# One attention and MLP kernel: the decay's shift moved into the exponential, its rows made and sent in another way, and an accumulation reordered

## The chip, the cores and the metric

The kernel runs on one core of one Trainium2 chip. The metric is device time in microseconds (us) of one execution; lower is better. A core has five engines that run their own instruction queues side by side: TensorE (PE, with its weight loads as PEld), VectorE (DVE), ScalarE (ACT), GpSimd (POOL) and SyncE (SP, which here only issues DMA transfers). They wait for each other by semaphores. Matrix results go to PSUM, a memory of eight banks; everything else lives in SBUF, 128 partitions wide.

## The reference

A "forgetting" attention is followed by a two-layer MLP. There are 8 batches, 8 heads, 576 positions and 64 features a head.

```python
log_f = np.log(np.clip(f, 0.0001, 1.0))
cum = np.cumsum(log_f, axis=-1)
decay = cum[:, :, :, None] - cum[:, :, None, :]
scores = np.where(causal, -1e9, q @ k.T / 8 + decay)      # per batch and head
attn = softmax(scores)
x = (attn @ v) as (4608, 512)                             # heads side by side
h = x @ w_in                                              # 512 -> 2048
out = (h - np.tanh(h)) @ w_out                            # 2048 -> 512, float32
```

The softmax is computed without its maximum: a fixed SHIFT of 5.0 is subtracted from each score ahead of the exponential instead, and it cancels in the division.

## The kernel before, in words

**Decay inside the matmul.** The score tile is K-rows times Q-columns, contracted over the 64 features. The decay is added by three more contraction rows: K carries a high part of 8·cum (rounded to fp16), the low part that the rounding left, and ones; Q carries minus one, minus one, and 8·cum - 40 (the 40 is 8·SHIFT). After the scale of 1/8 in the exponential that gives score + cum(i) - cum(j) - 5. So `QT` and `KT`, the operands of one batch, have D + 3 = 67 rows for each head; two sets of them alternate between batches.

**How the rows are made.** `f` is read in as 64 rows, one for each batch and head (L138), and a second time as 24 rows, three for each head of batch 0 (L139). VectorE clips them (L185), ScalarE takes the logarithm (L192), VectorE scans the prefix sums (`cum`, L195), then makes the high part `chi` (L197) and the low part. Per-row factors that pick high, low and one come from small operations on columns of an identity (`per`, L179 to L191). `cq`, ScalarE's 8·cum - 40 (L585), is the row for Q. From `chi`, `clo` and `cq` the rows are sent by DMA into `KT` and `QT`: by GpSimd's queue for batch 0 (`bulk`, L219 to L221), by SyncE's for the others (`load_aug`, L207); rows of plus and minus one are sent by SyncE too (`const_rows`).

**Pair 0.** Heads are worked on in pairs, 4 to a batch. The first pair cannot wait for those transfers. It has operands of its own, `KS` and `QS`, which borrow the space of later weights (`W1`, `W2`): 64 features and the 24 rows, 88 in all, written in place by the engines. For head 0, L198 writes K's rows and `row_q(0, ...)` (L580) the Q rows; head 1 gets a copy of K's rows (L593) and a second `row_q`, with other factors that pick its three rows of the 24.

**Start.** `start()` writes out by hand the order around it. TensorE first runs dummy matmuls on a constant tile (`unread`), then transposes q and k of pair 0 (`trans`, L304), then more dummies up to the first score tile (L358). Each transposed pair is copied from PSUM to SBUF in four parts (q by ScalarE, L315; k by VectorE, L317), so that head 0's two parts can come first. Each score tile is masked by a matmul with `late` in batch 0 (L361), and ScalarE's exponential (L367) takes it out of PSUM. There are seven tiles in a pair: 0 to 2 for the first head, 3 for the last keys of both heads, 4 to 6 for the second. `bulk()` then gives GpSimd its loads in order: q and k of heads 4 and 5, the three row transfers, q and k of heads 6 and 7, and v.

**After that.** `att_items(p)` gives the order of steps for each pair p: score tiles, transposes for the next pair, the products with v of the pair before (`values`, L395, with VectorE's division into `xn`), and for batch 1 on a DMA transpose of `xn` into `XR` (L429, L431), the transposed attention. MLP steps are dealt out in between by fixed counts: `mlp1` (L457) is one tile of 128 hidden features for a unit of 512 tokens, followed by ScalarE's tanh (L462) and VectorE's `gq` (L468). Of the nine units the first has a plain second layer (`mlp2_plain`, L498): a bank holds two blocks m of 128 tokens by 256 outputs; each block is summed in two steps of eight feature tiles, the first and the second half of the 2048. The order of its 16 steps is e (output half), mp (pair of token blocks), m, half. The other units save a multiplication of blocks by sums and differences (`mlp2`, L523). Engines run their instructions strictly in the written order; nothing is rescheduled. Each DMA queue of GpSimd takes eight transfers at a time: the ninth issue waits for the landing of the first.

Of the kernel before, what the change touches and what calls it, by code (L numbers as in the profile page):

```python
# [8 lines left out]
FP32 = mybir.dt.float32  # L9
FP16 = mybir.dt.float16  # L10
# [4 lines left out]
PITCH = 640  # L15
# [6 lines left out]
def kernel(  # L22
# [137 lines left out]
    clo = cst.tile([NH, S], FP16)  # L160
    cq = cst.tile([NH, S], FP16)
    KS = W1.rearrange("p k e -> p (k e)")[:, 0:2 * PITCH].rearrange("p (a n) -> p a n", a=2)
    QS = W2.rearrange("p k e -> p (k e)")[:, 0:2 * S].rearrange("p (a n) -> p a n", a=2)
    nc.vector.memset(KS[0:NX, :, S:PITCH], 0.0)
    per = cst.tile([NX, 9], FP32)
    nc.vector.memset(vn[0][D:P, NJ - 1, :, :], 0.0)
    isb, isc, mul_k, add_k, mul_l, mul_0, add_0, mul_1, add_1 = (per[:, i:i + 1] for i in range(9))
# [7 lines left out]
    def column(g, h):  # L175
        return id16[0:NX, NH + 3 * h + g:NH + 3 * h + g + 1]
# [11 lines left out]
    for h, (mul, add) in enumerate(((mul_0, add_0), (mul_1, add_1))):  # L188
        nc.vector.tensor_scalar_mul(out=mul, in0=column(1, h), scalar1=inv_qscale)
        nc.vector.scalar_tensor_tensor(out=add, in0=mul, scalar=-SHIFT, in1=column(0, h), op0=ALU.mult, op1=ALU.add)  # L190
        nc.vector.tensor_tensor(out=add, in0=add, in1=column(2, h), op=ALU.subtract)  # L191
# [6 lines left out]
    nc.vector.scalar_tensor_tensor(out=KS[NH:NX, 0, 0:S], in0=cum[NH:NX, :], scalar=mul_l[NH:NX, :], in1=chi[NH:NX, :],  # L198
                                   op0=ALU.mult, op1=ALU.subtract)

    def aug_rows(b):
        i, hs = b % 2, slice(b * H, (b + 1) * H)
        return [(KT[i][D:D + 1, :, 0:S], chi[hs, :]), (KT[i][D + 1:D + 2, :, 0:S], clo[hs, :]), (QT[i][D + 2:D + 3, :, :], cq[hs, :])]
# [5 lines left out]
    def const_rows(i):  # L209
        nc.sync.dma_start(out=QT[i][D:D + 2, :, :], in_=minus16)  # L210
        nc.sync.dma_start(out=KT[i][D + 2:D + 3, :, 0:S], in_=ones16[0:H, :])
# [3 lines left out]
    def bulk():  # L215
        (k_hi, chi_0), (k_lo, clo_0), (q_hi, cq_0) = aug_rows(0)
        load_qk(qn, q, 0, 4, 6)
        load_qk(kn, k, 0, 4, 6)
        nc.gpsimd.dma_start(out=k_hi, in_=chi_0)  # L219
        nc.gpsimd.dma_start(out=q_hi, in_=cq_0)  # L220
        nc.gpsimd.dma_start(out=k_lo, in_=clo_0)  # L221
# [121 lines left out]
    def scores(b, c, ti):  # L343
# [10 lines left out]
        kt, qt, rows = (KS, QS, NX) if b == 0 and c == 0 else (KT[b % 2], QT[b % 2], D + 3)  # L354
# [12 lines left out]
        nc.scalar.activation(out=e[:, lo:hi], in_=ps[:, lo:hi], func=AF.Exp, scale=qscale)  # L367
# [124 lines left out]
    def mlp2_plain(u, s):  # L492
        e, mp, m, half = s // 8, s // 4 % 2, s // 2 % 2, s % 2
# [82 lines left out]
    REST = []  # L576

    def start():
        def row_q(h, mul, add):
            nc.scalar.activation(out=QS[NH:NX, h, :], in_=cum[NH:NX, :], func=AF.Identity, bias=add[NH:NX, :], scale=mul[NH:NX, :])  # L580

        unread(47)
        row_q(0, mul_0, add_0)
        q_rest = trans(*pairs[0], qn, (QS,), True, "AAAA", True)
        nc.scalar.activation(out=cq, in_=cum[0:NH, :], func=AF.Copy, bias=-SHIFT * inv_qscale, scale=inv_qscale)  # L585
# [6 lines left out]
        nc.vector.scalar_tensor_tensor(out=clo, in0=cum[0:NH, :], scalar=inv_qscale, in1=chi[0:NH, :], op0=ALU.mult, op1=ALU.subtract)  # L592
        nc.vector.tensor_copy(out=KS[NH:NX, 1, 0:S], in_=KS[NH:NX, 0, 0:S])  # L593
# [13 lines left out]
    def att_items(p):  # L607
# [8 lines left out]
        for ti in range(len(TILES)):  # L616
# [5 lines left out]
            if p == 0 and ti in (0, 2, 5, 6):  # L622
                put(unread, {0: 2, 2: 14, 5: 4, 6: 6}[ti])
# [103 lines left out]
```

## Time and profile before

| | |
|---|---|
| median of 3 runs | 341.31 us (341.13 to 341.52) |
| the profiled execution's own time | 341.6 us |
| its span, first to last instruction | 339.9 us |
| granted TensorE clock | 1.00 |
| VectorE busy, share of the span | 77% |
| ScalarE busy | 69% |
| GpSimd busy | 48% |
| transfers in GpSimd's queue | 18.39 MB in 94592 packets |

The profile is of one execution. Instructions are grouped by line, engine and operation; a row of the timeline has its start, its duration, the engine, the line, what it writes and reads, how many instructions are merged, and in brackets how long the engine was idle before and what ended that. In the list of waits each row gives the total, how often, and the longest. The chain of waits is followed back from the last instruction; each piece has its start and length. In a stretch's row the first two numbers are its bounds and length, followed by busy time (and instruction count) of PE, PEld, DVE, ACT and POOL, the granted clock, the time the DMA engines were busy, and the rate. For DMA issues the last number is the median time from issue to landing. For one tile, a row gives the least, median and greatest of these times.

### The profile page before, as it was taken

The page shows a single profiled execution, that of the slowest core. Times are in us where ns is not written, and L with a number is a line of the kernel's source. Part 1 is how long each engine was busy: PE and PEld are TensorE (multiplying, and loading weights), DVE is VectorE, ACT ScalarE, POOL GpSimd, SP SyncE. Part 2 cuts the span into 40 slices and gives each one's busy share as a digit, 9 for nine tenths or more (in the row PEclk, how much of TensorE's full clock was granted, in tenths as well). Part 3 has the DMA queues.
Part 4 walks back from the last instruction along what each step waited for, and adds up shares of the span by engine and source line. Part 5 has one row for each costly group of instructions (what it writes and reads, how often), then busy time and mean ns, then how long its engine had stood idle before and what let it go on. Part 6 is the DMA issues. An engine that isn't in the chain of part 4 may idle for free.

```text
span 339.9 us, 8804 instructions
## 1 busy us (share of the span) xinstructions
PE 333.0 (98%) x3345; PEld 237.7 (70%) x3345; DVE 262.5 (77%) x516; ACT 235.1 (69%) x440; POOL 163.7 (48%) x323
## 2 busy tenths in 40 slices
PE   8999999999999999999999999999999999999995
PEld 8775557875588558855788888656875686486485
DVE  8898986659888888678967886688668766966864
ACT  6998777878987886778677867787558743632630
POOL 8894765885657573677377647632322210000000
PEclk9999999999999999999999999999999999999999
DMA  9999999999959999999999999990130023002003
GB/s 116 124 173 201 187 198 179 153 162 196 137 93 181 159 116 92 136 168 130 106 106 191 131 110 112 165 133 15 49 115 13 17 62 101 0 31 95 1 16 109
DMA packets 147535, 38.88 MB, mean 114 GB/s; under 512 B 128221, under 2 KB 146381, under 8 KB 147493
## 3 DMA queue, kind: packets, MB, share of 16 engines
q0 software_dynamic: 94592, 18.39, 74.1%
q1 hardware_dynamic: 52868, 19.88, 31.7%
q8 instruction: 26, 0.43, 0.5%
q14 instruction: 17, 0.13, 0.2%
q10 hardware_dynamic: 32, 0.06, 0.0%
HBM read 36.90 MB, written 9.44 MB: 136 GB/s over the span
## 4 chain that ended last, share of the span: by engine, by line
PE 85%; DVE 8%; DMA 2%; ACT 2%; issue 1%; ACTq 0%
PE hps L457 35%; PE ops L523 29%; PE ps L358 11%; PE av L395 7%; DMA XR<-xn 2%; PE ops L498 2%; DVE KT L317 2%; DVE QT L317 1%; ACT e L367 1%; DVE gq L468 1%; PE t L304 1%; DVE xn L406 1%; DVE W L317 1%; PE x L423 0%; DVE TQ L195 0%
## 5 line engine op out<-in xcount | busy, mean ns | idle before, releaser
L457 PE MATMUL hps<-XR,win 128*128 128x512 f16 (+1 forms) x640 | 140.9, 357 | 0.5 <-DMA XR<-xn 0.3
L462 ACT ACTIVATE th<-hps 128x512 f32<-128x512 f32 x144 | 86.6, 602 | 55.5 <-PE hps L457 52.8
L367 ACT ACTIVATE e<-ps 128x512 f16<-128x512 f32 x192 | 110.5, 598 | 9.8 <-PE ps L358 7.9
L468 DVE TENSOR_TENSOR gq<-hps,th 128x512 f16<-128x512 f32 x144 | 98.1, 687 | 24.2 <-ACT th L462 22.6
L377 POOL TENSOR_SCALAR_AFFINE_SELECT e<-e 128x128 f16<-128x128 f16 x168 | 60.3, 362 | 69.9 <-ACT e L367 67.9
L457 PEld LDWEIGHTS <-win 128*128 128x128 f16 x640 | 57.7, 97 | 48.7 <-issue 0.7
L358 PE MATMUL ps<-QT,KT 67*128 67x512 f16 (+1 forms) x372 | 73.8, 277 | 0.8 <-ACT e L367 0.4
L523 PEld LDWEIGHTS <-gq 128*128 128x128 f16 x640 | 60.2, 97 | 11.2
L523 PE MATMUL ops<-wout,gq 128*128 128x256 f16 x512 | 63.2, 272 | 0.0
L358 PEld LDWEIGHTS <-KT 67*128 67x128 f16 x372 | 35.3, 98 | 22.2 <-issue 1.2
L395 PEld LDWEIGHTS <-e 128*128 128x128 f16 x896 | 32.3, 97 | 3.6
L395 PE MATMUL av<-vn,e 128*128 128x65 f16 x896 | 33.6, 193 | 0.0
L131 POOL DMA_DIRECT2D vn<-in_v_dram x32 | 28.0, 878 | 7.5 <-DMA win<-in_moe_w_in_dram 3.4
L523 PE MATMUL ops<-W,sq 128*128 128x256 f16 x256 | 31.2, 272 | 0.0
L406 DVE TENSOR_TENSOR xn<-av,rs 128x640 f16<-128x640 f32 x32 | 26.4, 825 | 1.1
L523 PEld LDWEIGHTS <-sq 128*128 128x128 f16 x256 | 24.1, 97 | 3.4
L108 POOL DMA_DIRECT2D qn<-in_q_dram x25 | 21.1, 845 | 3.7 <-DMA wout<-in_moe_w_out_dram 1.9
L377 POOL TENSOR_SCALAR_AFFINE_SELECT el<-el 128x128 f16<-128x128 f16 x28 | 9.4, 337 | 26.9 <-ACT el L367 26.7
L108 POOL DMA_DIRECT2D kn<-in_k_dram x25 | 21.1, 845 | 1.5 <-issue 1.1
L404 DVE TENSOR_SCALAR rs<-av 128x10 f32<-128x10 f32 x32 | 5.2, 162 | 18.1 <-PE av L395 17.0
L498 PE MATMUL ops<-wout,gq 128*128 128x256 f16 x128 | 16.9, 272 | 0.4 <-DVE gq L468 0.3
L317 DVE COPY QT<-t 64x576 f16<-64x576 f16 x18 | 14.4, 801 | 3.5 <-PE t L304 3.4
(93 smaller groups left out, 321.0 us busy)
## 6 DMA issues: line engine op xcount, KB each, us to landing
out_dram<-ost SPq DMA_DIRECT2D x34, 256.0 KB
vn<-in_v_dram POOLq DMA_DIRECT2D x24, 128.0 KB, 5.6
qn<-in_q_dram POOLq DMA_DIRECT2D x20, 128.0 KB, 4.9
kn<-in_k_dram POOLq DMA_DIRECT2D x20, 128.0 KB, 5.0
win<-in_moe_w_in_dram POOLq DMA_DIRECT2D x2, 1024.0 KB, 12.3
wout<-in_moe_w_out_dram POOLq DMA_DIRECT2D x2, 1024.0 KB, 17.0
XR<-xn SPq DMA_TRANSPOSE x56
qn<-in_q_dram POOLq DMA_DIRECT2D x6, 144.0 KB, 4.7
```

What stands on the lines that cost most here:

```text
L108: nc.gpsimd.dma_start(out=dst[b % 2][0:pn, n, :].rearrange("p (h d) -> p h d", h=H), in_=src[b, :, n * P:n * P + pn, :].rearrange("h p d - ...
L131: nc.gpsimd.dma_start(out=vn[b % 2][:, n, h0:h1, 0:D], in_=v[b, h0:h1, n * P:(n + 1) * P, :].rearrange("h p d -> p h d"))
L317: nc.vector.tensor_copy(out=to, in_=of)
L358: nc.tensor.matmul(out=ps[:, col:col + n], lhsT=kt[0:rows, h, j * P:(j + 1) * P], rhs=qt[0:rows, h, i0:i0 + n], start=True, stop=cut == 0)
L367: nc.scalar.activation(out=e[:, lo:hi], in_=ps[:, lo:hi], func=AF.Exp, scale=qscale)
L377: nc.gpsimd.affine_select(out=view, in_=view, compare_op=ALU.is_ge, fill=0.0, base=0, pattern=pat, channel_multiplier=-1)
L395: nc.tensor.matmul(out=av[:, a, ib, :], lhsT=E.pop((b, c, a, j, ib)), rhs=vn[b % 2][:, j, 2 * c + a, 0:D + 1], start=(j == 0), stop=(j == ib))
L406: nc.vector.tensor_tensor(out=xn.rearrange("p i (a d) -> p a i d", a=2), in0=av[:, :, :, 0:D], in1=rs.to_broadcast([P, 2, NJ, D]), op=ALU. ...
L457: nc.tensor.matmul(out=hps[:, o:o + n], lhsT=win[:, ci, ft * P:(ft + 1) * P], rhs=XR[:, ci, t:t + n], start=(ci == 0), stop=(ci == NCH - 1))
L462: nc.scalar.activation(out=th, in_=hps, func=AF.Tanh, scale=-1.0)
L468: nc.vector.tensor_tensor(out=GQ[(u, i)][:, half, kt, :], in0=hps, in1=th, op=ALU.add)
L523: nc.tensor.matmul(out=ps[:, m, :], lhsT=LHS[lhs](u, kt // 4)[:, kt % 4, m * P:(m + 1) * P], rhs=rhs[:, kt, :], start=(fresh and (apart or ...
```

## The change

- SHIFT goes out of the Q rows and into the exponential, as a bias of -5.0 given as a number. Q's decay row is then 8·cum, and its fp16 form is K's high part `chi`: `cq` is dropped, and `chi` is sent to `QT` as well.
- The 24 extra rows of `f` become three, all of batch 0's head 0: partitions 64, 65 and 66 hold K's high, low and one row where `KT` wants them. The low parts of all rows are made by one operation (`clo`, 67 rows), and three rows of it are copied to head 0 of `KT`. `KS`, `QS` and the second `row_q` go; pair 0 uses `KT[0]` and `QT[0]`. Head 1 of pair 0, like heads 2 to 7, now gets its rows by DMA.
- `bulk` sends the three rows ahead of q and k of heads 4 and 5.
- All four q copies of pair 0 stand in ScalarE's queue ahead of the first exponential.
- Dummy matmuls between score tiles: 4, 4, 2 and 14 become 2 and 6.
- `mlp2_plain` runs both token blocks over the first half of the features before the second half.

```diff
-    NX = NH + 3 * H
+    NX = NH + 3
-    nc.scalar.dma_start(out=lf[NH:NX, :], in_=bass.AP(f.tensor, f.offset, [[S, H], [0, 3], [1, S]]))
+    nc.scalar.dma_start(out=lf[NH:NX, :], in_=bass.AP(f.tensor, f.offset, [[0, 3], [1, S]]))
...
-    for to, g in ((isb, 1), (isc, 2)):
-        nc.vector.tensor_reduce(out=to, in_=id16[0:NX, NH + g:NX:3], op=ALU.add, axis=mybir.AxisListType.X)
-    nc.vector.tensor_scalar(out=mul_k, in0=isb, scalar1=-inv_qscale, scalar2=inv_qscale, op0=ALU.mult, op1=ALU.add)
-    nc.vector.tensor_scalar_mul(out=add_k, in0=isb, scalar1=-1.0)
-    nc.vector.tensor_scalar_mul(out=mul_l, in0=isc, scalar1=inv_qscale)
+    r_hi, r_one = (id16[0:NX, NH + g:NH + g + 1] for g in (0, 2))
+    nc.vector.tensor_scalar(out=both, in0=r_one, scalar1=-inv_qscale, scalar2=inv_qscale, op0=ALU.mult, op1=ALU.add)
+    nc.vector.tensor_scalar_mul(out=add_k, in0=r_one, scalar1=-1.0)
+    nc.vector.scalar_tensor_tensor(out=mul_k, in0=r_hi, scalar=-2.0 * inv_qscale, in1=both, op0=ALU.mult, op1=ALU.add)
+    nc.vector.scalar_tensor_tensor(out=mul_l, in0=r_hi, scalar=-inv_qscale, in1=both, op0=ALU.mult, op1=ALU.add)
+    nc.vector.tensor_scalar_mul(out=mul_q, in0=r_one, scalar1=inv_qscale)
+    nc.vector.tensor_scalar_add(out=add_q, in0=r_one, scalar1=-1.0)
...
-    for h, (mul, add) in enumerate(((mul_0, add_0), (mul_1, add_1))):
-        nc.vector.tensor_scalar_mul(out=mul, in0=column(1, h), scalar1=inv_qscale)
-        nc.vector.scalar_tensor_tensor(out=add, in0=mul, scalar=-SHIFT, in1=column(0, h), op0=ALU.mult, op1=ALU.add)
-        nc.vector.tensor_tensor(out=add, in0=add, in1=column(2, h), op=ALU.subtract)
...
-    nc.vector.scalar_tensor_tensor(out=KS[NH:NX, 0, 0:S], in0=cum[NH:NX, :], scalar=mul_l[NH:NX, :], in1=chi[NH:NX, :],
-                                   op0=ALU.mult, op1=ALU.subtract)
+    nc.vector.scalar_tensor_tensor(out=clo, in0=cum, scalar=mul_l, in1=chi, op0=ALU.mult, op1=ALU.subtract)
+    nc.vector.tensor_copy(out=KT[0][NH:NX, 0, 0:S], in_=clo[NH:NX, :])
...
     def bulk():
-        load_qk(qn, q, 0, 4, 6)
-        load_qk(kn, k, 0, 4, 6)
         nc.gpsimd.dma_start(out=k_hi, in_=chi_0)
-        nc.gpsimd.dma_start(out=q_hi, in_=cq_0)
+        nc.gpsimd.dma_start(out=q_hi, in_=chi_0)
         nc.gpsimd.dma_start(out=k_lo, in_=clo_0)
+        load_qk(qn, q, 0, 4, 6)
+        load_qk(kn, k, 0, 4, 6)
...
-        kt, qt, rows = (KS, QS, NX) if b == 0 and c == 0 else (KT[b % 2], QT[b % 2], D + 3)
+        kt, qt, rows = KT[b % 2], QT[b % 2], D + 3
...
-        nc.scalar.activation(out=e[:, lo:hi], in_=ps[:, lo:hi], func=AF.Exp, scale=qscale)
+        nc.scalar.activation(out=e[:, lo:hi], in_=ps[:, lo:hi], func=AF.Exp, bias=-SHIFT, scale=qscale)
...
-        e, mp, m, half = s // 8, s // 4 % 2, s // 2 % 2, s % 2
+        e, mp, half, m = s // 8, s // 4 % 2, s // 2 % 2, s % 2
...
     def start():
         unread(47)
-        row_q(0, mul_0, add_0)
-        q_rest = trans(*pairs[0], qn, (QS,), True, "AAAA", True)
-        nc.scalar.activation(out=cq, in_=cum[0:NH, :], func=AF.Copy, bias=-SHIFT * inv_qscale, scale=inv_qscale)
+        nc.scalar.activation(out=QT[0][NH:NX, 0, :], in_=cum[NH:NX, :], func=AF.Identity, bias=add_q[NH:NX, :], scale=mul_q[NH:NX, :])
+        q_rest = trans(*pairs[0], qn, QT, True, "AAAA", True)
+        for fn in q_rest:
+            fn()
         unread(6)
-        k_rest = trans(*pairs[0], kn, (KS,), True, "VVVV", True)
+        k_rest = trans(*pairs[0], kn, KT, True, "VVVV", True)
         unread(38)
-        q_rest[0]()
         scores(*pairs[0], 0)
-        unread(4)
-        nc.vector.scalar_tensor_tensor(out=clo, in0=cum[0:NH, :], scalar=inv_qscale, in1=chi[0:NH, :], op0=ALU.mult, op1=ALU.subtract)
-        nc.vector.tensor_copy(out=KS[NH:NX, 1, 0:S], in_=KS[NH:NX, 0, 0:S])
         for fn in k_rest:
             fn()
         scores(*pairs[0], 1)
-        row_q(1, mul_1, add_1)
-        unread(4)
-        q_rest[1]()
+        unread(2)
...
-            if p == 0 and ti in (0, 2, 5, 6):
-                put(unread, {0: 2, 2: 14, 5: 4, 6: 6}[ti])
+            if p == 0 and ti in (2, 5, 6):
+                put(unread, {2: 6, 5: 4, 6: 6}[ti])
```

More of the change, by code (lines that the diff above doesn't have):

```diff
@@ L159 @@
     chi = cst.tile([NX, S], FP16)
[L160 to L165, printed above, removed]
+    clo = cst.tile([NX, S], FP16)
+    per = cst.tile([NX, 6], FP32)
     nc.vector.memset(vn[0][D:P, NJ - 1, :, :], 0.0)
-    isb, isc, mul_k, add_k, mul_l, mul_0, add_0, mul_1, add_1 = (per[:, i:i + 1] for i in range(9))
+    mul_k, add_k, mul_l, mul_q, add_q, both = (per[:, i:i + 1] for i in range(6))
     EL = [cst.tile([P, 192], FP16, tag=f"el{i}", name=f"el{i}") for i in range(3)]
@@ L197 @@
     nc.vector.tensor_scalar(out=chi, in0=cum, scalar1=mul_k, scalar2=add_k, op0=ALU.mult, op1=ALU.add)
-    nc.vector.scalar_tensor_tensor(out=KS[NH:NX, 0, 0:S], in0=cum[NH:NX, :], scalar=mul_l[NH:NX, :], in1=chi[NH:NX, :],
-                                   op0=ALU.mult, op1=ALU.subtract)
+    nc.vector.scalar_tensor_tensor(out=clo, in0=cum, scalar=mul_l, in1=chi, op0=ALU.mult, op1=ALU.subtract)
+    nc.vector.tensor_copy(out=KT[0][NH:NX, 0, 0:S], in_=clo[NH:NX, :])
     def aug_rows(b):
-        i, hs = b % 2, slice(b * H, (b + 1) * H)
-        return [(KT[i][D:D + 1, :, 0:S], chi[hs, :]), (KT[i][D + 1:D + 2, :, 0:S], clo[hs, :]), (QT[i][D + 2:D + 3, :, :], cq[hs, :])]
+        i, h0 = b % 2, 0 if b else 1
+        hs = slice(b * H + h0, (b + 1) * H)
+        return [(KT[i][D:D + 1, h0:H, 0:S], chi[hs, :]), (KT[i][D + 1:D + 2, h0:H, 0:S], clo[hs, :]), (QT[i][D + 2:D + 3, h0:H, :], chi[hs, :])]
     def load_aug(b):
@@ L209, in const_rows @@
     def const_rows(i):
[L210 to L211 removed]
+        h0 = 1 - i
+        nc.sync.dma_start(out=QT[i][D:D + 2, h0:H, :], in_=minus16[0:2 * (H - h0), :])
+        nc.sync.dma_start(out=KT[i][D + 2:D + 3, h0:H, 0:S], in_=ones16[0:H - h0, :])
     const_rows(0)
     def bulk():
[L216 removed]
+        (k_hi, chi_0), (k_lo, clo_0), (q_hi, _) = aug_rows(0)
+        nc.gpsimd.dma_start(out=k_hi, in_=chi_0)
+        nc.gpsimd.dma_start(out=q_hi, in_=chi_0)
+        nc.gpsimd.dma_start(out=k_lo, in_=clo_0)
         load_qk(qn, q, 0, 4, 6)
         load_qk(kn, k, 0, 4, 6)
[L219 to L221 removed]
         load_qk(qn, q, 0, 6, H)
```

6 lines of the change are left out of this document (1 added, 5 removed).

## The prediction

> **What bounds the kernel now.** I read the page first, then the waits of TensorE, then the chain of waits through the first 75 us, and last the timeline wherever that chain leaves TensorE.
>
> ```profile
> PE 333.0 (98%) x3345; PEld 237.7 (70%) x3345; DVE 262.5 (77%) x516; ACT 235.1 (69%) x440; POOL 163.7 (48%) x323
> DMA  9999999999959999999999999990130023002003
> ```
>
> TensorE is busy for 333.0 of 339.9 us, so everything that can be won lies in the other 7 us, and in matmuls on `warm` that only fill waits. The DMA digits stand at 9 up to about 240 us: a transfer that starts earlier does not simply land earlier.
>
> ```profile
> PE hps L457 <- DMA XR<-xn: 0.3, 1, 0.3
> ```
>
> ```profile
> PEld L498 <- DVE gq L468: 0.9, 2, 0.5
> ```
>
> These are the waits of matmuls and of weight loads that the change can touch outside the start. No wait of a matmul over 0.15 us begins after 90 us, so what is won before that should arrive at the end. The start is read from the chain of waits:
>
> ```profile
> 5.25 1.28 DVE TQ L195
> ...
> 9.08 0.76 DVE clo L592
> ...
> 9.86 0.30 DVE W L593
> ...
> 14.47 0.39 PE ps L358
> ```
>
> From the prefix sum (5.25) to the first score tile of pair 1 (14.47) the chain lies on VectorE without a break. TensorE fills those waits with dummies. So the start is worth what VectorE's queue loses or gains, as long as nothing else comes late.
>
> **The change part by part.** *VectorE's queue up to pair 1.* The rows that carry it:
>
> ```profile
> 4.26 0.68 ACT L192 ACTIVATE TQ<-TQ 88x576 f32<-88x576 f32 x1 [0.55 <-DVE TQ L185]
> 5.09 0.15 DVE L191 TENSOR_TENSOR per<-per,id 88x1 f32<-88x1 f32 x1
> 5.17 1.35 DVE L195 TENSOR_TENSOR_SCAN TQ<-TK,TQ 88x576 f32<-88x576 f16 x1
> 7.24 0.81 DVE L198 SCALAR_TENSOR_TENSOR W<-TQ,per,chi 24x576 f16<-24x576 f32 x1
> 9.10 0.10 PEld L358 LDWEIGHTS <-W 88*128 88x128 f16 x1 [0.31 <-DVE W L317]
> 12.80 1.61 DVE L317 COPY KT<-t 64x576 f16<-64x576 f16 x2
> ```
>
> Before, the scan is followed by chi, the low rows (0.81), two K copies, `clo` (9.08 to 9.86: 0.78 with its gap), the copy of the rows to head 1 (0.31), two more K copies, then pair 1's four. After, one operation makes all low parts, so the 0.78 goes; a copy of 3x576 for head 0 takes the place of the 24x576 copy. No 3-row copy is in the trace. Per instruction the 24-row one is nearest, 0.30; the bounds are 0.15 (the small `per` operations) and 0.81 (L198, same row length). I take 0.30. It moves ahead of head 0's K copies, so the first score tile is 0.3 later against the scan, but pair 1 gets 0.78 earlier against it.
>
> The scan itself starts sooner. Six `per` operations that ran between the clip and the scan (ending with L191, 5.09 + 0.15 = 5.24) are gone; the scan then waits only for the logarithm, which ends at 4.26 + 0.68 = 4.94. That is 0.2 at once; ahead of the clip two reductions and a memset go and three small operations come, which is about even (0.2 either way). I take 0.15, bounds 0 and 0.4. With that the first score tile stands at 9.10 + 0.3 - 0.15 = 9.25, after the 38 dummies, and pair 1's at 14.47 - 0.78 - 0.15 = 13.55. **Start: 0.93 earlier by VectorE.**
>
> *ScalarE.* It loses `cq`, the second q row and their places in the queue:
>
> ```profile
> 7.42 0.99 ACT L315 ACTIVATE W<-t 64x288 f16<-64x288 f16 x2
> 8.43 0.68 ACT L585 ACTIVATE cq<-TQ 64x576 f16<-64x576 f32 x1
> 10.72 0.86 ACT L580 ACTIVATE W<-TQ,per 24x576 f16<-24x576 f32 x1
> ```
>
> After: one q row (0.86 from about 6.4), four q copies (0.99 for two), done near 9.3; the first exponential is ready at about 9.7. Then the exponentials run without the 0.86 + 0.5 that stood between the second and the third. This is cover for VectorE's gain, not a term: pair 0's last tiles follow its exponentials about a us sooner. The exponential's immediate bias I cost at nothing. L585 has a bias and a scale as immediates, L192 has a scale and bias left at their defaults, and both take 0.68 for 576 elements; in the built program the exponential still reads only `ps`. If it were read as an operand it would cost half of what L580's two operands cost over L585, (0.86 - 0.68) / 2 = 0.09 for each of 192, some 0.5 us on the few that lie on the chain.
>
> *Rows by DMA.* Head 1 of pair 0 now needs rows from GpSimd's queue; before, pair 1 was their first reader. Their place:
>
> ```profile
> 5.03 1.54 POOL L127 DMA_DIRECT2D vn<-in_v_dram  x2
> 8.06 0.57 POOL L219 DMA_DIRECT2D KT<-chi  x1
> 9.40 0.53 POOL L220 DMA_DIRECT2D QT<-cq  x1 [0.78 <-ACT cq L585]
> 10.12 0.51 POOL L221 DMA_DIRECT2D KT<-clo  x1 [0.19 <-issue]
> 11.77 0.10 PEld L358 LDWEIGHTS <-W 88*128 88x128 f16 x1
> ```
>
> ```profile
> vn<-in_v_dram POOLq DMA_DIRECT2D x3, 64.0 KB, 4.8
> ...
> KT<-chi POOLq DMA_DIRECT2D x1, 9.0 KB, 4.3
> KT<-clo POOLq DMA_DIRECT2D x1, 9.0 KB, 2.6
> ```
>
> Chi's two issues come right after chi (near 7.0 and 7.55), clo's at about 8.1, since clo is ready near 7.9. The second v load before them, issued at about 5.8, lands 4.8 later, 10.6, and the rows queue behind it: 10.7 to 10.9. TensorE reaches head 1's part of tile 3 (11.77 before) at about 11.0. What waits behind that weight load is pair 1's K transposes, which VectorE wants only when pair 1's Q copies are done (its K copies take 1.61, so 13.55 - 1.61, about 11.9). So the rows may land up to about 11.4 at no cost, and each us beyond costs a us. Bounds: 8.1 + 2.6 = 10.7 (nothing) and 8.1 + 4.3 = 12.4 (1.0, the whole start term). I take nothing, since the slow 4.3 stood behind two q and k loads that now come after. Those loads slip behind the rows, to about 8.6; pairs 2 and 3 read them from 13.8 on, 5.2 after the issue, and the next row has the least, median and greatest landing of the first three k loads:
>
> ```profile
> DMA to landing us min/median/max: 4.1/4.8/5.5
> ```
>
> *The first weights.* GpSimd no longer waits 0.78 for `cq`, so what it issues later comes that much sooner, but queued transfers follow only in part:
>
> ```profile
> win<-in_moe_w_in_dram POOLq DMA_DIRECT2D x1, 1024.0 KB, 10.6
> ```
>
> ```profile
> 17.68 0.86 POOL L228 DMA_DIRECT2D win<-in_moe_w_in_dram  x1
> 28.91 0.81 PE L457 MATMUL hps<-XR,win 128*128 128x512 f16 x3
> ```
>
> It lands at 28.3, 0.6 ahead of its first matmul. If it comes 0.3 earlier, the start's gain is held to 0.9 here; if it doesn't move, to 0.6; if it moves by all of 0.78, there is no limit. **Start term: 0.9, bounds 0.6 and 1.3.**
>
> *Sixteen dummies fewer* (4+4+2+14 become 2+6): not a term, they only filled VectorE's chain.
>
> *Banks by feature halves.* In the first unit's second layer, step 1 now reads the first half of the features for the second token block, where before it read the second half for the first:
>
> ```profile
> 52.36 1.19 PE L498 MATMUL ops<-wout,gq 128*128 128x256 f16 x7
> 52.53 1.28 DVE L468 TENSOR_TENSOR gq<-hps,th 128x512 f16<-128x512 f32 x2
> 53.86 0.28 PE L498 MATMUL ops<-wout,gq 128*128 128x256 f16 x1 [0.32 <-DVE gq L468]
> 54.46 1.04 PE L498 MATMUL ops<-wout,gq 128*128 128x256 f16 x8
> ```
>
> The eight matmuls of step 1 take 52.36 to 54.14, 1.78, where an undisturbed eight takes 1.04: 0.74 goes. The new late reader, step 2, would start near 53.7 on this clock; its last matmul needs the feature tile that VectorE ends at 53.81, and comes after it. Bounds 0.32 (the matmul's own wait) and 0.9 (both waits of the weight loads, quoted above); I take 0.6, since VectorE ends that tile only just in time.
>
> *Later.* The transposed attention of batch 1 is the next thing TensorE waits for:
>
> ```profile
> 67.83 7.57 DMA XR<-xn
> ```
>
> ```profile
> 75.45 0.38 PE L457 MATMUL hps<-XR,win 128*128 128x512 f16 x1 [0.27 <-DMA XR<-xn]
> ```
>
> The chain goes from xn straight into the transposes, and xn moves with TensorE; the 7.57 run through busy queues. I take 0.1 of loss, bounds 0.27 of gain and all that was won.
>
> **Sum:** 0.9 + 0.6 - 0.1 = 1.4. The profiled execution took 341.6 us (span 339.9, 1.7 around it), 0.3 over the median of 341.31. So 340.2 for such an execution, **339.9** as a median.
>
> A rule that speaks against the change, weighed on this row:
>
> ```profile
> 9.10:14.47 5.37, 5.03 (x68) 3.98 (x69) 5.19 (x8) 5.13 (x11) 4.88 (x8) 1.00 0.95 123
> ```
>
> The granted clock is 1.00 here, with TensorE busy 5.03 of 5.37 us. Fewer dummies leave about the same 0.3 to 0.6 of idle time in 4.3 us, in pieces under 0.5. The Trainium skill, "TensorE: Matmul & The Clock Gate", Part 1, says that the clock is halved after about one idle window of 3.4 us, and Part 4 that transposes do not count as busy in the same way. By the first of these the sum stays, since no pause nears 3.4 us; by the second, with twelve transposes among few dummies, the clock could fall. No stage of this trace has a lower clock to show it, so it is a rival below.
>
> **The rivals.** *Eaten later.* The XR transposes, or the first weights, do not move. If XR lands at 75.4 whatever TensorE did, nothing is left: 341.2. For it: DMA at 9 everywhere. Against: the chain goes from xn straight into this transfer, so its issue moves along. Chance 0.20. *One term only.* Step 1's stall moves to step 2, or the start stops at 0.6: 0.6 to 0.9 in all, 340.6. Chance 0.15. *Slower: the rows land late.* Place: head 1's weight load in tile 3; price: one us for each us after 11.4; it outweighs 1.4 from 12.8 on, a landing 4.7 after clo's issue. The first loads took up to 5.5, and the next larger row is 10.6: at 6.4 (14.5) the loss is 3.1 against 1.4, so about 343.0. Against: 9 KB rows took 2.6 to 4.3 with more ahead of them. Chance 0.12. *Clock.* Were the granted clock halved from 9.25 to 13.55, the 4.3 us with TensorE busy for 5.03/5.37 of them, 4.0, would take 4.0 more: 341.3 - 1.4 + 4.0 = 343.9. Against: 1.00 in every stretch that I read. Chance 0.03. That the bias is not an immediate is in none: the program reads no operand.
>
> **How the numbers follow.** The forecast has 0.50. Measurements here tell about 0.2% (0.68 us) from no change: below 340.63 is faster, above 341.99 slower. Faster: 0.50 and most of the 0.15, 0.63. Same: the 0.20 and a little, 0.22. Slower: 0.15. The range goes from 339.0 (1.3 + 0.9 off the median is 339.1, and a little of the 0.27) to 341.4, which takes in the first two rivals and leaves out the slow ones.
>
> **What would show it.** Right: scan near 5.0, pair 1's first score tile near 13.5 behind a K copy of VectorE, step 1 of L498's successor in 1.04 with no wait on gq, XR waited for by under 0.5. Wrong: a weight load that waits for KT or QT by DMA near 11, a granted clock under 1.00 before 20 us, hps waiting for win near 28, a longer wait near 74, exponentials over 0.60.

## The result

The changed kernel takes **339.64 us** (median of 6 executions, 339.51 to 340.08); the kernel before took 341.36 beside it on the same chip (6, 341.10 to 341.52). The ratio is 0.9954, 95% interval 0.9941 to 0.9967: faster, by 1.72 us of the medians, which is half a percent. The forecast was 339.9. The profiled execution took 340.08, its span 338.4, so the profiles to compare differ by 1.5 (341.6 and 339.9 before).

The page of the changed kernel, against the busy row of before:

```profile
span 338.4 us, 8760 instructions
...
PE 331.6 (98%) x3329; PEld 237.4 (70%) x3329; DVE 261.1 (77%) x509; ACT 233.5 (69%) x438; POOL 162.6 (48%) x323
...
L361 ACT ACTIVATE e<-ps 128x512 f16<-128x512 f32 x192 | 110.4, 598 | 9.6 <-PE ps L352 7.0
```

TensorE has 16 matmuls and 1.4 us of work less; the dummies account for 1.1 of it (10.0 us in all against 11.1). The exponential with its immediate bias takes 598 ns.

TensorE's waits over 0.1 us in the changed kernel, after the 1.1 us ahead of its first dummy:

```profile
PE ps L352 <- ACT e L361: 0.6, 2, 0.4
PE ps L352 <- DMA KT<-clo: 0.6, 1, 0.6
PE hps L451 <- ACT XR L421: 0.2, 1, 0.2
```

Both waits of before that the prediction named are gone, the one for XR by DMA (0.3) and the one for `gq` (0.9 at the weight loads). A new one is there: 0.6 for `clo`'s rows. The timeline of the start shows where it lies:

```profile
4.20 0.68 ACT L184 ACTIVATE TQ<-TQ 67x576 f32<-67x576 f32 x1 [1.32 <-DVE TQ L181]
4.91 1.35 DVE L187 TENSOR_TENSOR_SCAN TQ<-TK,TQ 67x576 f32<-67x576 f16 x1 [0.66 <-ACT TQ L184]
7.76 0.30 DVE L191 COPY KT<-clo 3x576 f16<-3x576 f16 x1
8.21 0.51 POOL L213 DMA_DIRECT2D KT<-clo  x1
9.11 0.10 PEld L352 LDWEIGHTS <-KT 67*128 67x128 f16 x1 [0.27 <-DVE KT L311]
11.94 0.19 PE L352 MATMUL ps<-QT,KT 67*128 67x64 f16 x1 [0.58 <-DMA KT<-clo]
12.46 1.62 DVE L311 COPY KT<-t 64x576 f16<-64x576 f16 x2 [0.59 <-PE t L298]
13.72 0.50 PE L566 MATMUL idle<-warm 128*128 128x128 f16 x6
14.27 0.38 PE L352 MATMUL ps<-QT,KT 67*128 67x512 f16 x1
```

The scan starts 0.26 earlier than before (5.17). TensorE then stands in tile 3 until the rows of head 1 are there (11.94). Behind that matmul on its queue are pair 1's K transposes, so VectorE stands idle for 0.59 as well, and its K copies begin at 12.46 where 12.80 was before. The first tile of pair 1 comes at 14.27 against 14.47: 0.20 earlier, not 0.93. It follows six dummies (13.72), not a K copy (the last ends at 14.08), so by then more than VectorE's queue decides.

Further on, the timeline of the changed kernel has these places:

```profile
28.71 0.81 PE L451 MATMUL hps<-XR,win 128*128 128x512 f16 x3
52.18 1.04 PE L492 MATMUL ops<-wout,gq 128*128 128x256 f16 x8
53.53 1.04 PE L492 MATMUL ops<-wout,gq 128*128 128x256 f16 x8
74.35 1.89 PE L451 MATMUL hps<-XR,win 128*128 128x512 f16 x8
```

and the last of them before:

```profile
75.72 1.89 PE L457 MATMUL hps<-XR,win 128*128 128x512 f16 x8
```

Read as a lead over the kernel before, this says where the time went. First MLP matmul: 28.91 - 28.71 = 0.20. Step 1 of the plain second layer now takes 1.04 instead of 1.78, and the group of eight after it leads by 54.46 - 53.53 = 0.93, so the bank order gave 0.73. Past the place where TensorE waited for XR the lead is 75.72 - 74.35 = 1.37, another 0.44. At the end of the span it is 1.5.

**So the total is as forecast and its parts are not**: 0.20 + 0.73 + 0.44 and a last 0.1, against 0.9 + 0.6 - 0.1. Two questions are left: why the rows came late, and why the wait for XR went, which the prediction had at 0.1 of loss.

### The profile page after: what moved, and what is told of

Its sections match the earlier page's. It is cut to its first block, busy times and chain, and to the rows that moved or that the text cites. A ratio compares the mean times of both kernels' runs of the same rounds, so it can differ in the third digit from the quotient of the medians.

```text
span 338.4 us, 8760 instructions
## 1 busy us (share of the span) xinstructions
PE 331.6 (98%) x3329; PEld 237.4 (70%) x3329; DVE 261.1 (77%) x509; ACT 233.5 (69%) x438; POOL 162.6 (48%) x323
## 4 chain that ended last, share of the span: by engine, by line
PE 91%; DVE 2%; POOL 2%; ACT 2%; DMA 1%; issue 1%; ACTq 0%
PE hps L451 36%; PE ops L517 29%; PE ps L352 12%; PE av L389 8%; PE ops L492 4%; ACT e L361 2%; PE t L298 1%; DMA KT<-clo 1%; DVE KT L311 1%; DVE QT L311 0%; POOL vn L127 0%; POOL qn L102 0%; PE x L417 0%; POOL kn L102 0%; DVE xn L400 0%
## 5 line engine op out<-in xcount | busy, mean ns | idle before, releaser
L371 POOL TENSOR_SCALAR_AFFINE_SELECT e<-e 128x128 f16<-128x128 f16 x168 | 59.2, 356 | 72.5 <-ACT e L361 70.5
L352 PE MATMUL ps<-QT,KT 67*128 67x64 f16 (+4 forms) x384 | 76.5, 276 | 1.8 <-ACT e L361 0.6
L517 PEld LDWEIGHTS <-gq 128*128 128x128 f16 x640 | 60.3, 97 | 11.1
L517 PE MATMUL ops<-wout,gq 128*128 128x256 f16 x512 | 63.2, 272 | 0.0
L352 PEld LDWEIGHTS <-KT 67*128 67x128 f16 x384 | 36.5, 98 | 22.9 <-issue 1.3
L311 DVE COPY KT<-t 64x576 f16<-64x576 f16 (+1 forms) x20 | 14.7, 736 | 3.7 <-PE t L298 3.5
L532 ACT ACTIVATE m<-ops 128x512 f32<-128x512 f32 x16 | 9.5, 596 | 10.9 <-PE ops L517 10.9
```

The lines of the kernel that those rows point to most:

```text
L311: nc.vector.tensor_copy(out=to, in_=of)
L352: nc.tensor.matmul(out=ps[:, col:col + n], lhsT=kt[0:rows, h, j * P:(j + 1) * P], rhs=qt[0:rows, h, i0:i0 + n], start=True, stop=cut == 0)
L371: nc.gpsimd.affine_select(out=view, in_=view, compare_op=ALU.is_ge, fill=0.0, base=0, pattern=pat, channel_multiplier=-1)
L517: nc.tensor.matmul(out=ps[:, m, :], lhsT=LHS[lhs](u, kt // 4)[:, kt % 4, m * P:(m + 1) * P], rhs=rhs[:, kt, :], start=(fresh and (apart or ...
```

## The experiments

Each run is compared with runs of the kernel before on its own chip (medians 341.25 to 341.44).

**The two halves, alone.** The first theory: the bank order is worth its stall at step 1, the start some 0.2, and the wait for XR goes because of one of them. The rival: the start is worth most, and shows when alone. *bank_only* is the kernel before with the new order of steps; *no_bank* is the changed kernel with the old one.

```diff
 bank_only
-        e, mp, m, half = s // 8, s // 4 % 2, s // 2 % 2, s % 2
+        e, mp, half, m = s // 8, s // 4 % 2, s // 2 % 2, s % 2
 no_bank
-        e, mp, half, m = s // 8, s // 4 % 2, s // 2 % 2, s % 2
+        e, mp, m, half = s // 8, s // 4 % 2, s // 2 % 2, s % 2
```

> The kernel before, with only the order of the plain second layer's steps changed (both token blocks over the first half of the features first). Theory A (the bank order is worth a term of its own): step 1's eight matmuls take 1.04 us instead of 1.78, 0.74 is gained there, and the wait for XR near 75 us (0.27, 0.44 with the restart) goes or stays as the transposes land; 340.2 to 340.6 against 341.36 before. Rival B (the stall moves to step 2, whose last matmul needs the same feature tile): L498 keeps a wait on gq of 0.3 to 0.9, 341.2 to 341.4.

Measured for *bank_only*: 341.15 (11 executions, 340.52 to 341.41), ratio 0.9988 [0.9979, 0.9996]. The stall at step 1 is gone: the stretch from 50 to 56 us, first before, then here, has TensorE busy for 5.49 and 5.89 of 6 us.

```profile
50.00:56.00 6.00, 5.49 (x51) 3.85 (x49) 4.49 (x8) 3.92 (x7) 3.45 (x9) 1.00 1.46 198
```

```profile
50.00:56.00 6.00, 5.89 (x60) 4.62 (x58) 5.11 (x9) 4.66 (x8) 3.95 (x9) 1.00 1.45 198
```

Yet the median gains only 0.3. The timeline of *bank_only* shows where the rest is lost:

```profile
75.05 0.38 PE L457 MATMUL hps<-XR,win 128*128 128x512 f16 x1 [0.64 <-DMA XR<-xn]
75.32 1.89 PE L457 MATMUL hps<-XR,win 128*128 128x512 f16 x8
```

The wait for XR grew from 0.27 to 0.64. The matmuls just ahead of it and the issue of the transpose are both 0.76 earlier than before (73.60 against 74.36, 67.07 against 67.83), but the transpose takes 7.93 instead of 7.57, so XR lands only 0.40 earlier, and of a lead of 0.76 that much is left (75.72 - 75.32). The prediction's rival "eaten later" is thus half real here; in the changed kernel something else took it away.

> The changed kernel with the old order of the plain second layer's steps; only the start differs from before. Theory A (the rows' late landing left of the start's gain only what the traces show at the first MLP matmul, 28.91 against 28.71): 0.2 is gained at the start, step 1 stalls by 0.74 again, and the time is 341.0 to 341.3 against 341.36 before and 339.64 for the changed kernel. Rival B (the start brings most of the 1.7 us by way of transfers that come earlier later on, the XR transposes among them): 340.0 to 340.5.

Measured for *no_bank*: 340.91 (11, 340.61 to 341.72), ratio 0.9981 [0.9970, 0.9992], between the two forecasts. Its profiled execution took 340.99, 0.6 under that of before. The start is hardly a part of that: the first MLP matmul leads by 28.91 - 28.86 = 0.05 here, not 0.20. Behind XR the lead is 75.72 - 75.24 = 0.48: its list has no wait for XR by DMA, and the one for `gq` is back.

```profile
28.86 0.81 PE L451 MATMUL hps<-XR,win 128*128 128x512 f16 x3
```

```profile
PE ps L352 <- DMA KT<-clo: 0.4, 1, 0.4
PE ops L492 <- DVE gq L462: 0.3, 1, 0.3
```

So the start edits, not the bank order, took the XR wait away, though they moved TensorE by 0.05 to 0.20 us only.

**What took the XR wait away.** One DMA queue of the profile carries instructions: 26 packets of 16 KB in the changed kernel. TensorE has 3329 matmuls and as many weight loads there, 6658 instructions; 6658 / 26 = 256. I read the queue as TensorE's own code, one packet for about 256 instructions; the seventh packet, the one in question, begins when TensorE has begun 1729 to 1809 instructions in the six profiles compared here. In the DMA view of 70 to 74 us before and in *bank_only*, one packet falls among the XR transposes, and is slow: 3.7% of 16 engines over 4 us is 2.4 us on one engine, and 4.9% is 3.1.

```profile
q8 instruction: 1, 0.02, 3.7%
```

```profile
q8 instruction: 1, 0.02, 4.9%
```

In the changed kernel the packet, from 69 to 73 us, takes 1.0:

```profile
q8 instruction: 1, 0.02, 1.6%
```

The theory: a dummy matmul is two instructions (a weight load and a matmul), the change has 32 fewer, and so this packet is asked for later, when the transposes no longer wait for the engine that carries it. The rival: the start's other edits moved the transposes themselves. *bank_fewer* is *bank_only* with 16 dummies less at places before 10 us, and none of the start's other edits; *dummies_back* is the changed kernel with 16 more.

```diff
 bank_fewer (on bank_only)
-        unread(47)
+        unread(39)
-        unread(38)
+        unread(30)
 dummies_back
-                put(unread, {2: 6, 5: 4, 6: 6}[ti])
+                put(unread, {2: 22, 5: 4, 6: 6}[ti])
```

> The run with only the bank order, and 16 dummy matmuls fewer at the very start (39 instead of 47, and 30 instead of 38). In it and in the kernel before, TensorE's seventh instruction fetch (16 KB, at 70.7 and 71.8 us, taking 3.1 and 2.4 us) falls among the XR transposes and one DMA engine runs late; in the changed kernel it comes at 72.5, after them, and takes 1.0. Theory F (the 32 TensorE instructions fewer moved the fetch, and that took the wait for XR away): the fetch comes about 1.5 us later than at 70.7, TensorE waits for XR by under 0.2 instead of 0.64, 340.4 to 340.7 against 341.15 with the bank order alone. Rival D (earlier loads of GpSimd at the start are what made XR land sooner): the wait stays at 0.4 to 0.8, 341.0 to 341.3. The granted clock should stay 1.00, since no pause at the start grows past 1 us.

Measured for *bank_fewer*: 340.39 (12, 340.31 to 341.89), ratio 0.9974 [0.9966, 0.9983]. There is no wait for XR; the packet begins at 75.0, later than expected and behind the transpose. The transpose is issued 0.23 later than in *bank_only* (67.30) and lands 1.38 earlier (73.62 against 75.00). The group that stood still in *bank_only* runs through, and the lead over the kernel before, 0.55 ahead of this place (54.46 - 53.91), is 0.97 behind it (75.72 - 74.75):

```profile
73.83 1.03 PE L457 MATMUL hps<-XR,win 128*128 128x512 f16 x4
74.75 1.89 PE L457 MATMUL hps<-XR,win 128*128 128x512 f16 x8
```

Sixteen dummies of the first 10 us, which fill waits and compute nothing, are worth 341.15 - 340.39 = 0.76 us at 75 us.

> The changed kernel with its 16 dummies back, all between tiles 2 and 3 of pair 0 (22 instead of 6), where TensorE waits 0.58 for the rows. By themselves they cost about 16 x 0.06 - 0.58 = 0.4 at most. Theory F (the instruction count sets where the fetch falls): the seventh fetch comes at 71.2 to 71.8 among the XR transposes, a wait for XR of 0.2 to 0.7 is back, 340.2 to 340.7. Rival D: no wait for XR over 0.15, 339.6 to 340.1.

Measured for *dummies_back*: 340.43 (9, 340.40 to 341.54), ratio 0.9977 [0.9967, 0.9986], 0.8 above the changed kernel's median. The wait for XR is back:

```profile
74.76 0.38 PE L451 MATMUL hps<-XR,win 128*128 128x512 f16 x1 [0.23 <-DMA XR<-xn]
```

The 22 dummies also delay pair 1 by 0.31 themselves (first tile 14.58), so not all of the 0.8 is XR's. The packet begins at 72.3, later than expected, and takes only 1.3 (2.0% of 4 us), but it too falls ahead of the transpose's landing.

How the transpose lands shows what the packet does. Its landing is counted by 16 DMA engines. Before, 15 have counted by 74.02 and the last counts at 75.40; in *bank_only* 14 by 73.66 and two at 74.92 and 75.00; in *dummies_back* 14 by 73.64 and two at 74.65 and 74.72. In these three the packet begins (71.8, 70.7, 72.3) while the transpose runs. In the changed kernel, *no_bank* and *bank_fewer* it begins after all 16 have counted, and none is late (the last two counts lie 0.05 to 0.06 apart). So a packet amid the transpose goes with a delay of 1.0 to 1.4 us on one or two engines. *bank_fewer* carries the finding: with the start's other edits absent, the count of TensorE's instructions alone makes or removes the wait. A transfer with the packet moved and nothing else was not made. In the changed kernel and *no_bank* all engines also count some 1 us sooner after the issue than in the other four, which alone would have hidden such a delay; *dummies_back* loses that too, and why is open.

**Why the rows came late.** The prediction had them at 10.7 to 10.9. In the DMA view of 7 to 8.7 us of the changed kernel the last number is the time from issue to landing:

```profile
KT<-chi POOLq DMA_DIRECT2D x1, 7.9 KB, 4.2
QT<-chi POOLq DMA_DIRECT2D x1, 7.9 KB, 3.8
KT<-clo POOLq DMA_DIRECT2D x1, 7.9 KB, 3.6
```

8.21 + 3.6 = 11.8. The second v load lands at 10.88, and the three rows land one after the other behind it, at 11.32, 11.50 and 11.85. Their own packets are done by 10.1 in the trace; what comes late is the count of one of 16 engines (for the last of the three, 15 have counted by 11.3). The theory: they wait behind the v loads in GpSimd's queue. Two ways past it are SyncE's queue (*rows_sync*), and the v loads moved behind (*rows_before_v*: both; *rows_mid_v*: one). *rows_after_qk* undoes the diff's own order.

```diff
 rows_sync
-        nc.gpsimd.dma_start(out=k_hi, in_=chi_0)
+        nc.sync.dma_start(out=k_hi, in_=chi_0)
 (the same for q_hi and k_lo)
 rows_after_qk
+        load_qk(qn, q, 0, 4, 6)
+        load_qk(kn, k, 0, 4, 6)
         nc.gpsimd.dma_start(out=k_hi, in_=chi_0)
         nc.gpsimd.dma_start(out=q_hi, in_=chi_0)
         nc.gpsimd.dma_start(out=k_lo, in_=clo_0)
-        load_qk(qn, q, 0, 4, 6)
-        load_qk(kn, k, 0, 4, 6)
```

> The changed kernel with the three row transfers of batch 0 issued from SyncE's queue, directly after the rows of ones, instead of GpSimd's. Theory A (in the changed kernel the rows land late since they stand behind the loads of v in GpSimd's queue): they land near 10.2 to 10.5 instead of 11.85, the wait of 0.58 us in tile 3 goes, VectorE's K copies of pair 1 follow the Q copies without its 0.59 of idle time, pair 1's first tile runs near 13.6 instead of 14.27, and the time is 339.0 to 339.2. Rival B (small transfers take 3.6 us by whatever queue): tile 3 still waits 0.4 to 0.7, 339.5 to 339.8. Rival C (the rows come early, but exponentials and dummies hold pair 1): no wait in tile 3, pair 1's first tile still after 14.0, 339.4 to 339.8.

Measured for *rows_sync*: 343.89 (6, 342.86 to 344.58), ratio 1.0067 [1.0052, 1.0082]. All that was expected was wrong. TensorE gets its rows at 13.20, later than by GpSimd's queue (11.94):

```profile
13.20 0.19 PE L352 MATMUL ps<-QT,KT 67*128 67x64 f16 x1 [1.84 <-DMA QT<-chi]
```

And then the clock falls. In a stretch's row the number after POOL's busy time is the granted clock:

```profile
11.00:13.00 2.00, 0.30 (x4) 0.10 (x1) 0.85 (x2) 0.38 (x1) 2.00 (x4) 1.00 1.39 166
15.00:17.00 2.00, 1.94 (x17) 1.49 (x16) 0.33 (x1) 0.81 (x3) 2.00 (x4) 0.50 1.69 180
19.00:21.00 2.00, 2.00 (x33) 1.73 (x31) 1.58 (x2) 1.30 (x3) 2.00 (x3) 0.50 1.11 199
14.30:21.13 6.83, 6.62 (x70) 5.27 (x68) 4.22 (x6) 4.01 (x8) 6.72 (x12) 0.50 1.41 180
```

After two us with TensorE busy for 0.30, it runs at half clock, from 14.30 to 21.13. Why small transfers by SyncE's queue land later than GpSimd's wasn't followed up.

> The changed kernel with the row transfers again behind the q and k loads of heads 4 and 5 in GpSimd's queue. Theory A (tile 3 waits for the rows, one us for each us): clo's issue moves from 8.21 to about 9.6 and its landing from 11.85 to 12.6 to 13.2, the wait in tile 3 grows from 0.58 to 1.4 to 2.0 us, and the time is 340.4 to 341.0. Rival C (exponentials and dummies hold pair 1 anyway): the time changes by under 0.3, 339.5 to 339.9.

Measured for *rows_after_qk*: 343.52 (11, 341.08 to 344.68), ratio 1.0047 [1.0027, 1.0066]. The wait is as the theory had it:

```profile
13.15 0.19 PE L352 MATMUL ps<-QT,KT 67*128 67x64 f16 x1 [1.79 <-DMA QT<-chi]
```

Three executions, the profiled one among them, kept the clock at 1.00: 341.32, 341.26 and 341.08. So even these lie above the 340.4 to 341.0 that was expected, and a wait of 1.79 does not always bring the clock down. The other eight had a mean clock of 0.985 to 0.995 and took 342.78 to 344.68. So the order of `bulk` is worth some 1.6 us against the changed kernel while the clock holds, and 3 to 5 when it doesn't: it decides whether the change wins at all.

```diff
 rows_before_v (rows_mid_v: head 1's load alone, directly behind the rows)
-    load_v_head(0, 0)
-    load_v_head(0, 1)
...
     def bulk():
         (the three row transfers)
         load_qk(qn, q, 0, 4, 6)
         load_qk(kn, k, 0, 4, 6)
+        load_v_head(0, 0)
+        load_v_head(0, 1)
```

> The changed kernel with the two loads of v (heads 0 and 1 of batch 0) moved in GpSimd's queue from ahead of the row transfers to behind q and k of heads 4 and 5. Theory A (the rows wait behind those loads): the rows land at 10.4 to 11.2 instead of 11.85, the wait in tile 3 is under 0.2 instead of 0.58, VectorE's K copies start near 11.9 instead of 12.46, 339.0 to 339.3 against 339.64, unless v then comes late for the products with pair 0 near 15.3. Rival C (exponentials and dummies hold pair 1 anyway): no wait in tile 3, but 339.5 to 339.8. Rival B (3.6 us is what such a transfer takes): wait and time as in the changed kernel.

Measured for *rows_before_v*: 340.66 (11, 340.27 to 343.90), ratio 0.9989 [0.9975, 1.0003]. With neither of the two v loads ahead the last row lands 2.2 after its issue, at 10.44, TensorE doesn't wait for it, and VectorE's K copies begin at 11.89:

```profile
KT<-clo POOLq DMA_DIRECT2D x1, 7.9 KB, 2.2
```

```profile
11.89 1.61 DVE L311 COPY KT<-t 64x576 f16<-64x576 f16 x2
13.69 0.38 PE L352 MATMUL ps<-QT,KT 67*128 67x512 f16 x1
```

That is what the prediction's 0.9 wanted: K copies at about 11.9, and pair 1's first tile at 13.69 where it had 13.55. So 0.78 of the start's 0.93 comes when the rows are in time. But the last block of v is then late for pair 1's products, near 21.5 us, and the profiled execution lost its clock after that (0.50 from 21.8 to 28.6 us, 343.9; it is the only one of the eleven with a mean below 0.998):

```profile
PE av L389 <- DMA vn<-in_v_dram: 1.4, 1, 1.4
```

Late rows are traded for late v.

> The changed kernel with one of the two loads of v (head 1 of batch 0) moved from ahead of the row transfers to directly behind them. With both behind q and k of heads 4 and 5 the rows landed at 10.44 and tile 3 did not wait, but the last v block came 1.4 us late for pair 1, near 21. Theory A (one load fewer ahead brings the rows about 0.6 sooner): landing at 10.9 to 11.3 instead of 11.85, a wait in tile 3 of 0 to 0.2 instead of 0.58, later loads at most 0.8 later and the last v block by 19.5, in time: 339.0 to 339.4 against 339.64. Rival E (any load that moves behind the rows makes v late): a wait on vn of 0.3 to 1.5 near 20, 339.8 to 341, in some executions with a granted clock below 1.

Measured for *rows_mid_v*: 340.26 (12, 339.50 to 343.23), ratio 0.9975 [0.9958, 0.9992]. One v load fewer ahead of the rows does not bring them sooner:

```profile
11.93 0.19 PE L352 MATMUL ps<-QT,KT 67*128 67x64 f16 x1 [0.57 <-DMA KT<-clo]
```

The one load that is left ahead lands at 10.81, hardly sooner than the second of two (10.88), and the rows follow it as before. So the delay is not so much for each load in front. Two loads ahead or one: 3.6 from issue to landing; none: 2.2. Theory A missed; the time lies in rival E's range, but its wait for v isn't in the list. The median is 0.6 above the changed kernel's; two of the twelve executions have mean clocks of 0.990 and 0.995, and why the others are slower isn't shown. What makes the slowest engine late stays open.

**What the dummies are for.** *no_dummies* takes the dummies between the score tiles out, and pair 1's eight.

```diff
-        unread(2)
...
-            if p == 0 and ti in (2, 5, 6):
-                put(unread, {2: 6, 5: 4, 6: 6}[ti])
-            if p == 1 and ti == 6:
-                put(unread, 8, True)
```

> The changed kernel without the 26 dummies after the first score tile (2, 6, 4, 6 in pair 0 and 8 in pair 1). In the two kernels of the last batch whose rows came latest, a pause of 1.8 us was followed by a granted clock of 0.50 for 6 us, in most executions. Theory G (the clock falls by pauses, and here none reaches 1 us): clock 1.00, 339.3 to 339.7. Rival H (the share of work counts, and the dummies carry it): the granted clock falls below 0.9 somewhere from 11 to 22 us, and the time is 341 to 344.

Measured: 341.71 (12, 339.69 to 344.23), ratio 1.0008 [0.9988, 1.0028]. Eleven of twelve executions have a mean clock of 0.985 to 0.995; the twelfth, at 0.998, took 339.69, the time of the changed kernel. The stretches of the profiled execution:

```profile
11.00:13.00 2.00, 1.06 (x13) 0.77 (x14) 1.36 (x2) 1.00 (x3) 2.00 (x4) 0.95 1.09 149
13.00:15.00 2.00, 1.64 (x11) 0.99 (x11) 1.03 (x2) 1.54 (x4) 2.00 (x3) 0.50 1.47 148
17.00:19.00 2.00, 2.00 (x34) 1.73 (x32) 1.56 (x2) 1.30 (x3) 2.00 (x4) 0.50 1.33 177
```

TensorE waited 1.05 us for the rows and 0.38 for an exponential, and ran at half clock from 12.8 to 19.6 us. That is rival H's outcome. It doesn't refute G, which had assumed that no wait reaches 1 us. But the length of one wait does not decide: *bank_fewer* has a wait of 1.00 us and a clock of 0.998 or more in all twelve executions.

```profile
9.08 0.39 PE L358 MATMUL ps<-W,W 88*128 88x512 f16 x1 [1.00 <-DVE W L317]
```

The dummies that the change keeps save no work, they hold the clock.

**The bias as an operand.** Same kernel, with -5.0 read from a column.

```diff
+    shift = cst.tile([P, 1], FP32)
+    nc.vector.memset(shift, -SHIFT)
...
-        nc.scalar.activation(out=e[:, lo:hi], in_=ps[:, lo:hi], func=AF.Exp, bias=-SHIFT, scale=qscale)
+        nc.scalar.activation(out=e[:, lo:hi], in_=ps[:, lo:hi], func=AF.Exp, bias=shift, scale=qscale)
```

> The changed kernel with the exponential's bias read from a column of SBUF that holds -5.0 for each partition, instead of given as a number. By the rows of the kernel before, an operand costs (0.86 - 0.68) / 2 = 0.09 us for each exponential: mean 0.69 instead of 0.60, ScalarE busy 17 us longer over the span, and 0.3 to 1.5 us on the time, since a part of the exponentials up to 28 us lies on the chain: 339.9 to 341.2. Rival: the operand's fetch overlaps the exponential before, mean 0.60 to 0.62, time as in the changed kernel, 339.5 to 339.9.

Measured: 345.34 (4, 345.10 to 345.93), ratio 1.0116 [1.0101, 1.0131], 5.7 over the changed kernel.

```profile
L363 ACT ACTIVATE e<-ps,shift 128x512 f16<-128x512 f32 x192 | 127.1, 689 | 7.2 <-PE ps L354 5.1 <-POOL e L373 0.8 <-PE ps L357 0.5
```

```profile
PE ps L354 <- ACT e L363: 2.5, 10, 0.6
```

The exponential takes 689 ns, 91 more, as the prediction had worked out (0.09). The Trainium skill, "ScalarE: Activation LUTs", section "What ACT_TABLE_LOAD costs", gives about 93 ns for each operand read through a pointer; this run agrees. But the time was missed: 5.7 instead of 0.3 to 1.5. Three groups of the second layer, far apart, first in the changed kernel, then here (the two times behind the three durations are where a group starts and ends):

```profile
L517 PE MATMUL ops<-W,gq x16: 270/272/273, 103.5 to 105.6; 128*128 128x256 f16 x16
L517 PE MATMUL ops<-W,gq x16: 270/272/273, 209.8 to 211.8; 128*128 128x256 f16 x16
L517 PE MATMUL ops<-W,gq x16: 272/272/273, 279.2 to 280.8; 128*128 128x256 f16 x16
```

```profile
L519 PE MATMUL ops<-W,gq x16: 270/273/273, 106.0 to 108.3; 128*128 128x256 f16 x16
L519 PE MATMUL ops<-W,gq x16: 270/272/273, 214.6 to 216.9; 128*128 128x256 f16 x16
L519 PE MATMUL ops<-W,gq x16: 273/273/273, 285.1 to 286.7; 128*128 128x256 f16 x16
```

The lag is 2.5 at 104 us, 4.8 at 210 and 5.9 at 279. It grows from batch to batch as long as there are exponentials: 192 x 0.091 = 17.5 us are added to ScalarE, and a third of it arrives. The exponentials are on the path far more often than a list of TensorE's waits in the kernel before suggests; of the 5.8 by which the span grew that list names 1.9 at the exponentials (2.5 against 0.6) and some 1.0 at other waits of the start. Some 2.9 is in TensorE's busy time (334.5 against 331.6), where the profile doesn't say what it waited for.

## Why the prediction came out as it did

- **Right: direction, total, range.** 339.64 stands 0.3 under 339.9. But two misses cancel: the start gave 0.2 of 0.9, and "later" gave 0.44 to 0.5 where 0.1 of loss was forecast. That the total came so close is luck, and no proof of the sum.
- **The step that failed in the start** is the landing of the rows: "the second v load ... lands 4.8 later, 10.6, and the rows queue behind it: 10.7 to 10.9. ... I take nothing". The v load landed at 10.88, 0.3 later than that, and the last row 0.97 behind it instead of 0.1 to 0.3. That is 11.85, past the 11.4 up to which the rows were free by that same argument; TensorE waited 0.58. The bounds given there, 10.7 to 12.4, hold it; the value taken stood too near the good end. The price of one us for each us after 11.4 gives 0.45 of the 0.73 that is missing (0.93 - 0.20). In fact the K copies begin 0.61 after the landing, so the rows were free only up to about 11.3, and the copies stand 0.56 behind the 11.9 of the prediction. The rest lies between the K copies, which kept 0.34 of their lead (12.80 - 12.46), and the first tile of pair 1, 0.20: six dummies at 13.72 stand ahead of that tile, behind exponentials (waits of up to 0.4 in the list). *rows_before_v* shows the step's other half right: with the rows in time the K copies begin at 11.89 and the first tile at 13.69.
- **Right on VectorE's queue**: the 3x576 copy took 0.30 as taken, the scan gained 0.26 (0.15 taken, bounds 0 to 0.4), the first score tile stands at 9.11 (9.25).
- **Bank order**: mechanism right, 0.73 measured, 0.6 taken, 0.74 worked out from the rows. Step 2 didn't become the new late reader. The haircut had no row behind it.
- **"Sixteen dummies fewer: not a term" was wrong.** They moved TensorE's instruction packet out of the XR transposes, worth 0.76 between *bank_only* and *bank_fewer*. So the term "later" failed, 0.44 of gain where 0.1 of loss was taken. "The chain goes from xn straight into the transposes" was right for the issue and wrong as a reason that XR's landing moves along: in *bank_only* the issue came 0.76 earlier and the landing 0.40, since the 7.57 that was taken as given became 7.93. Without the packet's move, "eaten later" would have taken half of the bank's gain.
- **Immediate bias**: free, as said (598 ns, as before). Its counterfactual price was right for an instruction and wrong by ten for the kernel: instead of "the few that lie on the chain", a third of what all 192 add arrived.
- **Clock**: a chance of 0.03, and it didn't happen. "No pause nears 3.4 us" was the wrong comfort: in three profiles the clock was halved behind pauses of 1.05, 1.4 and 1.84 us. The changed kernel's 0.58 left it at 0.999 to 1.00, and nothing in the profile of before told how near it was.

None of the ten kernels' medians beats the changed one.

## What to carry to other kernels

Follow the lead of the new kernel over the old at a few fixed places (first MLP matmul, a layer's first group, the last wait, the end): it splits a total into terms, and shows when misses cancel. When a removed engine step makes a transfer's landing the next to decide, take the slow end of its bounds, and ask what pause it would leave TensorE in. Filler matmuls are not free of effect: here they held the clock, and their number decided when the next block of instructions was fetched.

## What the runs showed of the hardware

- **Instruction fetches share the DMA engines**, if the queue is read rightly. A packet of 16 KB for about 256 TensorE instructions took 1.0 us in one profile and 1.3 to 3.1 amid transposes. In three profiles the transposed tile then landed 1.0 to 1.4 us late on one or two of 16 engines; in three with the packet behind it on none.
- **The clock can halve after pauses far under 3.4 us**, and not in every execution. The profiles have 0.50 behind TensorE's waits of 1.84 us (*rows_sync*), 1.05 with 0.38 behind it (*no_dummies*) and 1.40 (*rows_before_v*). In *rows_after_qk* the profiled execution kept 1.00 behind 1.79 us. Mean clocks of 0.985 to 0.995 were in 6 of 6, 11 of 12, 1 of 11 (0.990) and 8 of 11 executions of these; with 0.58 in none of 6, with 0.57 (*rows_mid_v*) in 2 of 12, with 1.00 (*bank_fewer*) in none of 12.
- **The clock changes on a grid of 3.41 us.** In the three profiles each drop lasts 6.83 us, and it begins 10.24, 6.83 and 17.07 us after the trace's first record of the clock (4.06, 5.98 and 4.72 us), all multiples of 3.41. In the 3.41 us ahead of the drop TensorE was busy for 44, 65 and 57%. In *rows_after_qk* an edge of the grid (12.03) lies inside the wait, and the two parts have 69 and 62%. Which share decides stays open: 62% kept the clock and 65% lost it. The Trainium skill, "TensorE: Matmul & The Clock Gate", Part 1, has one idle window of 3.4 us as the condition, in windows that run freely and so differ from run to run. The runs agree with the windows, and not with the idleness of a whole one.
- **A small transfer lands with its slowest engine**: the rows' packets were done by 10.1, the landing was at 11.85.
